# Own loads, own casts, own order: plain fp32 loads on one queue with engine casts, a hand-ordered schedule, and folded weights built in 64x32 PE tiles

## The chip, the cores and the metric

The kernel runs on one core of a Trainium2 chip. The metric is the device time of one execution in microseconds (us), as the median of several executions. A profile covers one execution; its span is about 2 us shorter than the reported time of the same execution (319.5 us of span for 321.31 us before). Engine names: PE is the matrix engine, PEld its weight loads, DVE the vector engine, ACT the scalar engine, POOL the GpSimd engine, SP the engine that only issues DMAs here. A program on one core has no second die to compare with, so a single run is called fast or slow by the other runs of its kernel.

## The reference, cut to what matters

```python
# q, k, v: (8 batches, 8 heads, 576, 64)   p: (8, 8, 32, 64)   all fp32
p_packed = softmax(p k^T / 8) v                  # 32 packed rows per head
x        = softmax(q p_packed^T / 8) p_packed    # (8, 8, 576, 64) -> (4608, 512)
out      = relu(x @ w_in)**2 @ w_out             # w_in 512x2048, w_out 2048x512
```

Both kernels use an identity that makes the rest readable. The second attention has only 32 keys per head, so x @ w_in can be written as a2 @ M. Here a2 holds the 256 softmax columns (8 heads of 32), and M = p_packed @ w_in, folded per head, is 256x2048 for each batch. For each batch the kernels run the attention chain (k transposes, s1, pv, extraction of p_packed, M, s2, norm), then fc1 (a2 @ M, relu, square), then fc2 (the product with w_out). The attention chain of batch b+1 and the fc2 of batch b-1 are merged into the fc1 of batch b.

## The kernel before: the parts that matter

Loads go through the casting DMA queue (issued by POOL, fp32 in memory, bf16 when landed). Only v is loaded as fp32 and cast by POOL.

```python
def load_kqv(b):
    ...
    for qd in range(NQD):
        nc.gpsimd.dma_start(t.k[:, qd, :], quad(k, qd))        # casts on the way
    for jp in range(JP):
        nc.sync.dma_start(t.vf[32 * jp:32 * jp + 32], vv[jp])  # fp32, 32 partitions each
    for qd in range(NQD):
        nc.gpsimd.dma_start(t.q[:, qd, :], quad(q, qd))
...
setup()                               # p, memsets
loads = {0: load_kqv(0)}
for c in range(NWC): load_w_in(c)
loads[1] = load_kqv(1)
for c in range(NWC): load_w_out(c)
```

M is built in pairs of matmuls on two 128x64 halves of the PE array. Each contracts 128 rows with weights that are half zeros.

```python
def m(self, qd, c):
    ps = ps_att.tile([P, 512], F32, name="ps_a", tag="a")
    for pr in range(2):
        nc.tensor.matmul(ps[64 * pr:64 * pr + 64, :], lhsT=self.ppT[:, qd, pr, :],
                         rhs=w_in_b[:, qd * 2 + pr, c * WCH:(c + 1) * WCH], start=True, stop=True)
    # evacuated by ACT (qd 0) or DVE (qd 1), scaled by 1/denominator
```

fc1 is four matmuls, a relu on ACT and a square on DVE.

```python
nc.scalar.activation(r[:].rearrange("p (c n) -> p c n", c=2), ps[:, :, :HALF], ACT.Relu)
nc.vector.tensor_tensor(out=g[:, fb, o:o + S], in0=r, in1=r, op=ALU.mult)
```

The order of instructions on each engine is left to the tool's scheduler. The `merge` function only gives it the program order.

The softmax here doesn't subtract the row's maximum and nothing guards it: scores larger than these inputs give would overflow.

Of the kernel before, what the change touches and what calls it, by code (L numbers as in the profile page):

```python
# [9 lines left out]
F32 = mybir.dt.float32  # L10
# [17 lines left out]
def kernel_impl(tc, q, k, v, p, w_in, w_out, out):  # L28
# [14 lines left out]
    with ExitStack() as ctx:  # L43
        consts = ctx.enter_context(tc.tile_pool(name="consts", bufs=1))
        qkv = ctx.enter_context(tc.tile_pool(name="qkv", bufs=2))
        att = ctx.enter_context(tc.tile_pool(name="att", bufs=2))
        small = ctx.enter_context(tc.tile_pool(name="small", bufs=4))
        mpool = ctx.enter_context(tc.tile_pool(name="mpool", bufs=2))
        rpool = ctx.enter_context(tc.tile_pool(name="rpool", bufs=4))
        opool = ctx.enter_context(tc.tile_pool(name="opool", bufs=4))  # L50
# [6 lines left out]
        w_in_b = consts.tile([P, NCB, DFF], BF16, name="w_in_b")  # L57
# [3 lines left out]
        p_b = consts.tile([P, B * NQD, D], BF16, name="p_b")  # L61
        pT_bd = consts.tile([P, B * NQD, 2, P], BF16, name="pT_bd")
        ppT_bd = [consts.tile([P, NQD, 2, 64], BF16, name=f"ppT_bd{i}") for i in range(2)]
        pq_bd = [consts.tile([P, NQD, 2, P], BF16, name=f"pq_bd{i}") for i in range(2)]

        def load_kqv(b):
            t = Ctx()
            t.k = qkv.tile([P, NQD, JT * D], BF16, name="k_b")
            t.v = qkv.tile([JP * 32, G, H * D], BF16, name="v_b")
            t.vf = qkv.tile([JP * 32, H, G * D], F32, name="v_f")  # L70
            t.q = qkv.tile([P, NQD, JT * D], BF16, name="q_b")

            def quad(src, qd):
                return src[b, qd * QH:(qd + 1) * QH].rearrange("h (a j) d -> (h a) (j d)", j=JT)

            for qd in range(NQD):
                nc.gpsimd.dma_start(t.k[:, qd, :], quad(k, qd))  # L77
            vv = v[b].rearrange("h (a jp g) d -> jp a h (g d)", jp=JP, g=G)
            for jp in range(JP):
                nc.sync.dma_start(t.vf[32 * jp:32 * jp + 32], vv[jp])  # L80
            for qd in range(NQD):
                nc.gpsimd.dma_start(t.q[:, qd, :], quad(q, qd))  # L82
            return t

        def load_w_in(c):
            nc.gpsimd.dma_start(
                w_in_b[:, :, c * WCH:(c + 1) * WCH],
                w_in[:, c * WCH:(c + 1) * WCH].rearrange("(cb p) f -> p cb f", p=P))

        def load_w_out(c):  # L90
            nc.gpsimd.dma_start(
                w_out_b[:, c * 4:(c + 1) * 4, :],
                w_out[c * WCH:(c + 1) * WCH, :].rearrange("(fb p) e -> p fb e", p=P))

        def setup():
            nc.gpsimd.dma_start(p_b, p.rearrange("b (qd h) i d -> (h i) (b qd) d", h=QH))
            nc.vector.memset(pT_bd, 0.0)
            nc.vector.memset(ones_bd, 0.0)
            nc.vector.memset(ones_c, 1.0)
            for h in range(QH):  # L100
                nc.vector.memset(ones_bd[32 * h:32 * h + 32, 32 * h:32 * h + 32], 1.0)
            for i in range(2):
                nc.vector.memset(ppT_bd[i], 0.0)
                nc.vector.memset(pq_bd[i], 0.0)

        def setup_p(b):
            for h in range(QH):
                r = slice(32 * h, 32 * h + 32)
                for qg in range(b * NQD, (b + 1) * NQD):
                    nc.vector.transpose(  # L110
                        pT_bd[r, qg, :, r],
                        p_b[r, qg, :].rearrange("p (dh dl) -> p dh dl", dh=2))

        class Att:
            def __init__(self, b, t):
                self.b, self.t = b, t
                self.kT = att.tile([P, NQD, 2, S], BF16, name="kT")
                self.qT = att.tile([P, NQD, 2, S], BF16, name="qT")
# [4 lines left out]
                self.ppT = ppT_bd[b % 2]  # L123
                self.pq = pq_bd[b % 2]

            def tr_q(self, qd):
                nc.vector.transpose(  # L127
                    self.qT[:, qd].rearrange("p dh (j a) -> p j dh a", a=32),
                    self.t.q[:, qd, :].rearrange("p (j dh dl) -> p j dh dl", dh=2, dl=32))

            def tr_k(self, qd):
                nc.vector.transpose(  # L132
                    self.kT[:, qd].rearrange("p dh (g jp a) -> p jp g dh a", jp=JP, a=32),
                    self.t.k[:, qd, :].rearrange("p (jp g dh dl) -> p jp g dh dl", jp=JP, dh=2, dl=32))

            def cast_v(self, qd):
                nc.gpsimd.tensor_copy(  # L137
                    self.t.v[:, :, qd * QH * D:(qd + 1) * QH * D].rearrange("p g (h d) -> p h g d", d=D),
                    self.t.vf[:, qd * QH:(qd + 1) * QH, :].rearrange("p h (g d) -> p h g d", d=D))

            def s1(self, qd, hf):
                ps = ps_att.tile([P, 512], F32, name="ps_a", tag="a")
                for gi in range(3):
                    g = hf * 3 + gi
                    for dh in range(2):
                        lhsT = self.kT[:, qd, dh, g * 96:(g + 1) * 96]
                        nc.tensor.matmul(ps[:JP * 32, gi * P:(gi + 1) * P], lhsT=lhsT,  # L147
                                         rhs=pT_bd[:, self.b * NQD + qd, dh, :],
# [4 lines left out]
            def pv(self, qd):  # L153
# [3 lines left out]
                c0 = qd * 256  # L157
                for pr in range(2):
                    h0 = qd * QH + 2 * pr
                    for g in range(G):  # L160
# [60 lines left out]
            def steps(self):  # L221
# [3 lines left out]
                for qd in range(NQD):  # L225
                    for hf in range(2):
                        st.append(lambda qd=qd, hf=hf: self.s1(qd, hf))
# [133 lines left out]
```

## Time and profile before

| before | value |
|---|---|
| reported time, median of 4 | 321.25 us (321.07 to 321.68) |
| span of the profile, PE busy | 319.5 us, 80% |
| first M matmul | 56.88 us |
| first relu of fc1, batches 0, 1, 2 | 66.7, 90.5, 116.1 us |
| first relu of fc1, batch 7, and end | 277.0, 319.5 us |

The page of the profile cuts the span into 40 slices of 8.0 us. A digit is a busy share in tenths. The PEclk row is the clock granted to PE in tenths of full speed (it shows 9 also where the trace holds no clock record, here before 63.5 us), and GB/s is what the DMA engines moved.

```profile
PE   0030200889999999999979998999999999999994
...
POOL 7032715141041311130030012000000000000000
PEclk9999999979999999999999999999999999999999
DMA  9999999994097364555442321121111111112232
GB/s 160 198 212 209 213 256 210 240 192 74 3 194 157 61 148 102 135 100 124 112 101 43 96 64 33 34 54 49 34 33 35 33 36 50 48 35 66 52 81 67
```

PE is nearly empty for seven slices while the DMA row is full, then nearly full to the end. The chain of waits (start, length, what) says which loads the first stage waited for:

```profile
4.62 19.37 DMA w_in_b<-in_moe_w_in_dram
24.28 15.86 DMA w_out_b<-in_moe_w_out_dram
40.66 16.19 DMA k_b<-in_k_dram
```

The timeline of DVE shows the second reason for the late start. The transposes of p for later batches stand ahead of batch 0's extraction (the reciprocal):

```profile
38.67 8.52 DVE L110 STREAM_TRANSPOSE pT_bd<-p_b 32x64 bf16<-32x64 bf16 x45
47.22 0.17 DVE L171 RECIPROCAL rD<-ps_pp 128x2 f32<-128x2 f32 x1
```

From the starts of successive matmuls in the trace, the nominal step is 216 ns for a 512-column matmul, 122 for 288, 56 for 128, and 29 for 64. A pair of M matmuls starts 3 ns apart, but the step before it grows from 216 to 309 ns and the step after it is 336 ns. A pair thus costs 309 - 216 + 3 + 336 = 432 ns, about half of which is not streaming. This is as the Trainium skill (TensorEngine Tiling (Array Packing), Key Properties) has it: a change of tiling mode drains the engine.

### The profile page before, as it was taken

How to read it: one execution, taken by the hardware profiler on the slowest of the kernel's cores; microseconds unless marked ns; L12 is line 12 of the kernel's file. 1: busy time of each engine (PE TensorE's matmuls, PEld its weight loads, DVE VectorE, ACT ScalarE, POOL GpSimd, SP SyncE). 2: the span in 40 equal slices, each digit the busy share in tenths (PEclk: the TensorE clock that was granted, in tenths of full speed). 3: DMA queues.
4: the chain of work that ended last, by engine and by line, in shares of the span. 5: the costliest groups of instructions: out<-in, count | busy, mean ns of one | idle time of the engine just before them, and what ended most of it. 6: DMA issues, size and time to landing. Idle time of an engine off the chain costs nothing.

```text
span 319.5 us, 4844 instructions
## 1 busy us (share of the span) xinstructions
PE 256.6 (80%) x1792; PEld 140.4 (44%) x1792; DVE 164.9 (52%) x355; ACT 178.9 (56%) x357; POOL 48.2 (15%) x61
## 2 busy tenths in 40 slices
PE   0030200889999999999979998999999999999994
PEld 0030200256464456445634564546445644455441
DVE  3073894569685966484648464842454245433100
ACT  1020001768887855785579556856785578565211
POOL 7032715141041311130030012000000000000000
PEclk9999999979999999999999999999999999999999
DMA  9999999994097364555442321121111111112232
GB/s 160 198 212 209 213 256 210 240 192 74 3 194 157 61 148 102 135 100 124 112 101 43 96 64 33 34 54 49 34 33 35 33 36 50 48 35 66 52 81 67
DMA packets 24360, 33.09 MB, mean 104 GB/s; under 512 B 5392, under 2 KB 15632, under 8 KB 24336
## 3 DMA queue, kind: packets, MB, share of 16 engines
q0 software_dynamic: 10896, 13.90, 26.3%
q1 hardware_dynamic: 13440, 18.89, 23.9%
q8 instruction: 14, 0.23, 0.3%
q14 instruction: 10, 0.08, 0.1%
HBM read 37.22 MB, written 9.44 MB: 146 GB/s over the span
## 4 chain that ended last, share of the span: by engine, by line
PE 66%; DMA 16%; DVE 8%; ACT 6%; issue 1%; POOL 1%; ACTq 0%; POOLq 0%
PE ps_o L263 34%; PE ps_h L247 17%; PE ps_a L190 7%; DMA w_in_b<-in_moe_w_in_dram 6%; DMA k_b<-in_k_dram 5%; DMA w_out_b<-in_moe_w_out_dram 5%; PE ps_a L147 3%; ACT r L251 3%; DVE gT L253 3%; PE ps_a L203 3%; DVE a_641 L219 1%; PE ps_a L214 1%; PE ps_pp L161 1%; DVE kT L132 1%; DVE qT L127 1%
## 5 line engine op out<-in xcount | busy, mean ns | idle before, releaser
L263 PE MATMUL ps_o<-w_out_b,gT 128*128 128x512 bf16 x576 | 156.3, 380 | 0.0
L251 ACT ACTIVATE r<-ps_h 128x576 bf16<-128x576 f32 x128 | 82.4, 648 | 37.2 <-PE ps_h L247 35.8
L253 DVE TENSOR_TENSOR gT<-r 128x576 bf16<-128x576 bf16 x128 | 59.7, 472 | 67.7 <-ACT r L251 66.9
L263 PEld LDWEIGHTS <-gT 128*128 128x128 bf16 x576 | 52.4, 98 | 44.6 <-issue 8.9
L247 PEld LDWEIGHTS <-M 128*128 128x128 bf16 x512 | 48.4, 98 | 30.5 <-issue 5.5
L197 DVE TENSOR_SCALAR M<-ps_a,rD 128x512 bf16<-128x512 f32 x32 | 24.0, 750 | 22.8 <-PE ps_a L190 22.5
L132 DVE STREAM_TRANSPOSE kT<-k_b 128x1152 bf16<-128x1152 bf16 x16 | 22.0, 1376 | 26.5 <-DMA k_b<-in_k_dram 23.6
L147 PE MATMUL ps_a<-pT_bd,kT 128*96 128x128 bf16 x192 | 17.5, 238 | 20.5 <-DVE pT_bd L110 20.4
L267 ACT COPY o_sb<-ps_o 128x512 f32<-128x512 f32 x36 | 21.0, 584 | 20.4 <-PE ps_o L263 20.1
L137 POOL CAST v_b<-v_f 96x1536 bf16<-96x1536 f32 x16 | 23.8, 1522 | 53.7 <-DMA v_f<-in_v_dram 28.1
L147 PEld LDWEIGHTS <-kT 128*96 128x96 bf16 x192 | 16.2, 138 | 25.0 <-DVE kT L132 19.5
L203 PE MATMUL ps_a<-qT,pq_bd_94 128*128 128x288 bf16 x32 | 7.6, 323 | 22.5 <-ACT pq_bd_94 L183 19.5
L195 ACT ACTIVATE M<-ps_a,rD 128x512 bf16<-128x512 f32 x32 | 22.0, 688 | 5.8 <-PE ps_a L190 5.0
L183 ACT ACTIVATE pq_bd_94<-ps_pp 32x64 bf16<-32x64 f32 x16 | 3.4, 213 | 33.9 <-DVE ppT_bd_92 L174 26.3
L127 DVE STREAM_TRANSPOSE qT<-q_b 128x1152 bf16<-128x1152 bf16 x16 | 21.6, 1362 | 0.6 <-PE ps_a L203 0.6
L190 PE MATMUL ps_a<-w_in_b,ppT_bd_92 128*64 128x512 bf16 x64 | 14.1, 434 | 2.0 <-ACT M L195 1.2
L216 ACT ACTIVATE ls<-ps_a 128x288 f32<-128x288 f32 x32 | 13.4, 418 | 4.0 <-PE ps_a L214 3.5
L218 ACT ACTIVATE rs<-ls 128x288 f32<-128x288 f32 x32 | 14.2, 445 | 0.8
L82 POOL DMA_DIRECT2D q_b<-in_q_dram x16 | 8.5, 536 | 40.8 <-DVE qT L127 33.7
L203 PEld LDWEIGHTS <-pq_bd_94 128*128 128x128 bf16 x32 | 3.0, 101 | 26.2 <-ACT pq_bd_94 L183 21.0
L161 PEld LDWEIGHTS <-v_b 96*128 96x128 bf16 x192 | 8.2, 101 | 13.1 <-POOL v_b L137 11.4
L77 POOL DMA_DIRECT2D k_b<-in_k_dram x16 | 8.5, 536 | 32.9 <-DVE kT L132 23.8
(165 smaller groups left out, 236.3 us busy)
## 6 DMA issues: line engine op xcount, KB each, us to landing
v_f<-in_v_dram SPq DMA_DIRECT2D x24, 384.0 KB, 7.0
out_dram<-o_sb SPq DMA_DIRECT2D x144, 64.0 KB, 1.7
k_b<-in_k_dram POOLq DMA_DIRECT2D x16, 288.0 KB, 13.2
q_b<-in_q_dram POOLq DMA_DIRECT2D x16, 288.0 KB, 9.7
w_in_b<-in_moe_w_in_dram POOLq DMA_DIRECT2D x4, 512.0 KB, 20.3
w_out_b<-in_moe_w_out_dram POOLq DMA_DIRECT2D x4, 512.0 KB, 18.7
p_b<-in_p_dram POOLq DMA_DIRECT2D x1, 256.0 KB, 15.2
```

Of the source, the lines that this page charges most:

```text
L127: nc.vector.transpose(self.qT[:, qd].rearrange("p dh (j a) -> p j dh a", a=32), self.t.q[:, qd, :].rearrange("p (j dh dl) -> p j dh dl", d ...
L132: nc.vector.transpose(self.kT[:, qd].rearrange("p dh (g jp a) -> p jp g dh a", jp=JP, a=32), self.t.k[:, qd, :].rearrange("p (jp g dh dl) ...
L137: nc.gpsimd.tensor_copy(self.t.v[:, :, qd * QH * D:(qd + 1) * QH * D].rearrange("p g (h d) -> p h g d", d=D), self.t.vf[:, qd * QH:(qd + 1 ...
L147: nc.tensor.matmul(ps[:JP * 32, gi * P:(gi + 1) * P], lhsT=lhsT, rhs=pT_bd[:, self.b * NQD + qd, dh, :], start=(dh == 0), stop=(dh == 1))
L190: nc.tensor.matmul(ps[64 * pr:64 * pr + 64, :], lhsT=self.ppT[:, qd, pr, :], rhs=w_in_b[:, qd * 2 + pr, c * WCH:(c + 1) * WCH], start=True ...
L195: nc.scalar.activation(dst, ps, ACT.Copy, scale=self.rD[:, qd:qd + 1])
L197: nc.vector.tensor_scalar_mul(dst, ps, self.rD[:, qd:qd + 1])
L247: nc.tensor.matmul(ps[:, c, :HALF], lhsT=a.M[:, qd, fb * FB:(fb + 1) * FB], rhs=a.a2[:, qd, c * HALF:(c + 1) * HALF], start=(qd == 0), sto ...
L251: nc.scalar.activation(r[:].rearrange("p (c n) -> p c n", c=2), ps[:, :, :HALF], ACT.Relu)
L253: nc.vector.tensor_tensor(out=g[:, fb, o:o + S], in0=r, in1=r, op=ALU.mult)
L263: nc.tensor.matmul(st.ps, lhsT=g[:, fb, n0:n0 + P], rhs=w_out_b[:, fb, :], start=(fb == 0), stop=(fb == NFB - 1))
L267: nc.scalar.copy(o_sb, st.ps)
```

## The change

The intent has four parts. First, start earlier: load only what batch 0 needs first, on one plain queue, in the order of need. Second, since plain loads don't cast, let POOL, ACT and DVE cast. Third, take the order of every engine into one's own hands (`manual_schedule`, with weights for where each list is merged). Fourth, build M in groups of eight matmuls on eight 64x32 tiles (64 rows of contraction, without the zeros), so 32 groups in place of 64 pairs. The q-side scale moves, and the layouts of k and v change so that v can be loaded in two pieces of 96 partitions; for this the k transposes write with a stride of 3 elements.

The core of the diff, cuts marked with `...`:

```diff
+        ctx.enter_context(tc.manual_schedule())
         ...
+            def dma_kq(self, name, qd):
+                src = {"k": k, "q": q}[name]
+                f = stg.tile([P, JT * D], F32, name="kq_f", tag="kq")      # 4 staging buffers
+                nc.sync.dma_start(f, src[self.b, qd * QH:(qd + 1) * QH].rearrange(
+                    "h (a j) d -> (h a) (j d)", j=JT))
         ...
+            def cast_kq(self, name, qd, engs):
+                ...
+                t = qkv.tile([P, JT * D], BF16, name=name + "_b", tag="kqb")
+                for i, e in enumerate(engs):
+                    cast(e, t[:, i * n:(i + 1) * n], f[:, i * n:(i + 1) * n])
         ...
+        def dma_w_out(c):
+            f = stg.tile([P, 2, NE], F32, name="w_f", tag="w", bufs=4)
+            nc.sync.dma_start(f, w_out[c * 2 * P:(c + 1) * 2 * P, :].rearrange("(fb p) e -> p fb e", p=P))
+            w_f[c] = f
+        def cast_w_out(c, eng):
+            cast(eng, w_out_b[:, 2 * c:2 * c + 2, :], w_f[c])
         ...
-                    self.kT[:, qd].rearrange("p dh (g jp a) -> p jp g dh a", jp=JP, a=32),
+                    self.kT[:, qd].rearrange("p dh (g a jp) -> p jp g dh a", jp=JP, a=32),
         ...
-            def m(self, qd, c):
-                ps = ps_att.tile([P, 512], F32, name="ps_a", tag="a")
-                for pr in range(2):
-                    nc.tensor.matmul(ps[64 * pr:64 * pr + 64, :], lhsT=self.ppT[:, qd, pr, :],
-                                     rhs=w_in_b[:, qd * 2 + pr, c * WCH:(c + 1) * WCH],
+            def m(self, c):
+                pss = [ps_att.tile([P, 512], F32, name="ps_a", tag="a") for _ in range(NQD)]
+                for h in range(QH):
+                    for qd in range(NQD):
+                        pr, e = divmod(h, 2)
+                        o = 32 * (h ^ qd)
+                        nc.tensor.matmul(pss[qd][o:o + 32, :], lhsT=self.ppT[64 * e:64 * e + 64, qd, pr, :],
+                                         rhs=w_in_b[64 * e:64 * e + 64, qd * 2 + pr, c * WCH:(c + 1) * WCH],
         ...
+        merge([([lambda fb=fb: fc1_unit(a0, fb) for fb in range(8)], 0, 1), (c1, 0, 1)])
+        cast_w_in(1, 3, V)
+        a0.m(2)
+        a0.m(3)
         ...
+        merge([(pc[4:], 0.0, 0.02), ([s1[4], s1[7]] + s1[8:], 0.0, 0.25), (fst, 0.06, 0.55),
+               ([lambda fb=fb: fc1_unit(a1, fb) for fb in range(NFB)], 0.25, 0.75), (rest, 0.55, 1),
+               (pool_casts(L[2])[:2] + [lambda: prep_p(2, B)] + pool_casts(L[2])[2:], 0.55, 0.7),
+               (a2.steps(), 0.6, 1.0), (L[3].dma_steps(), 0.6, 0.9)])
```

In the last call each list has the stretch (0 to 1) of the merged program in which its steps are spread.

## The prediction

> **What bounds the kernel now.** Two stages. (1) Start-up: in the 40 slices PE is nearly empty until slice 8; the chain of waits is DMA from 4.6 to 56.9 us (w_in 19.4, w_out 15.9, k 16.2 us), and the timeline has the first M matmul at 56.9 us. It is order rather than bandwidth: v of two batches and all of w_out are among the first loads, k lands only at 17.8 us, and the scheduler put 45 transposes of p (8.5 us) and those of batch 1 ahead of batch 0's extraction, which waits until 47.2 us. (2) From 57 us PE: 39 to 40 of 40 us busy per window. Start-to-start times from the trace: fc2 216 ns, fc1 122, s1 56, pv 29. An M pair (128x64 tiles) runs together, but stretches the matmul before it from 216 to 309 ns and needs 336 itself: 432 ns per pair, 27.6 us for 64 pairs, half of it switching. That agrees with the Trainium skill (TensorEngine Tiling (Array Packing), Key Properties): changing the tiling mode drains the engine. PE work is about 30.7 us per batch, 245 in all; ACT and DVE are at 70% and 50%.
>
> **Loads.** The casting queue writes 2304-byte packets in 192 ns, 205 to 210 GB/s written, so some 420 GB/s read. Perfetto Trace Analysis, Roofline, in the skill, gives about 435 for 16 engines: plain fp32 loads read the same bytes and win almost no bandwidth. They win order: p of two batches, k0, v0, q0 and half of w_in are 5.8 MB, an estimated 15 to 17 us. With casts (POOL about 1 ns per element per partition, from the v cast's 1.5 us), transposes (1.4 us) and the extraction, the first M matmul comes at about 21 us (18 to 27). The other weights and batch 1 (about 10 MB, 25 us) land by about 45 us, so up to 50 us PE runs with holes: I allow 8 us. Casts add about 8 us per batch to POOL, which has room.
>
> **M.** 64 pairs become 32 groups of eight 64x32 matmuls on eight different tiles. If all stream together, a group costs 216 + 213 + some loads, about 480 ns: 15 us instead of 27.6. If the two row halves take turns, about 21.
>
> **Sum.** PE work 29.2 us per batch, 233 us, 4 of it before the first M. 21 + 229 + 8 (holes while loading) + 5 (steady holes; before has about 10 there) = 263; + 4.6 from last matmul to the end of the span (as before) - about 2 if hand order is tight; + 1.7 between span and reported time. About **266 us**, range 252 to 281. Faster by over 2%: 0.97; within 2%: 0.02; slower: 0.01. Of the 55 us, 28 are start-up (36 less 8), 12 M, the rest scheduling.
>
> **What would show it.** Timeline: first M at 18 to 27 us; extraction before 18. DMA row: full to about 45 us, 350 to 420 GB/s instead of 200. M: from a group's first matmul to the next instruction near 340 ns rather than 550. PE nearly full from 50 us. ACT busiest after PE, about 80% of steady time.
>
> **What would make it wrong.** Row halves not overlapping (+6 us); the SP queue shared by loads that wait for staging buffers and stores behind them, so an output buffer could hold ACT and then PE; POOL casts slowed by DVE so that k/q come late; both attention PSUM buffers taken by one M group, so each next step waits for the slower of ACT and DVE; w_out later than 45 us.

## More of the kernel before

From the groups of instructions, three lines are needed later. Columns: line, engine, operation, output<-input, shapes, count; then busy us and mean ns; then idle time before them and what ended it.

```profile
L253 DVE TENSOR_TENSOR gT<-r 128x576 bf16<-128x576 bf16 x128 | 59.7, 472 | 67.7 <-ACT r L251 66.9
L132 DVE STREAM_TRANSPOSE kT<-k_b 128x1152 bf16<-128x1152 bf16 x16 | 22.0, 1376 | 26.5 <-DMA k_b<-in_k_dram 23.6
L137 POOL CAST v_b<-v_f 96x1536 bf16<-96x1536 f32 x16 | 23.8, 1522 | 53.7 <-DMA v_f<-in_v_dram 28.1
```

The windows view gives the busy time of each engine in a stretch. The two rows are fc1 of batch 0 to 1 and of batch 1 to 2:

```profile
66.00:90.00 24.00, 23.20 (x180) 13.75 (x179) 17.40 (x36) 19.83 (x42) 5.15 (x7) 0.93 0.42 76
90.00:116.00 26.00, 24.80 (x195) 13.99 (x194) 21.17 (x37) 20.78 (x44) 7.08 (x8) 1.00 0.74 150
```

The columns are window, its length, busy us (and count) of PE, PEld, DVE, ACT and POOL, clock, DMA share, GB/s. PE is busy 23.2 of 24 us and 24.8 of 26 us: once it started, this kernel hardly had holes, even while the second half of the loads was landing.

## The result, and the profile after

| | before | after |
|---|---|---|
| reported time, median (lowest to highest), 4 runs each | 321.25 (321.07 to 321.68) | 309.74 (308.44 to 310.8) |
| ratio of fast runs, 95% interval | 1 | 0.9638 (0.9599 to 0.9677) |
| first M matmul | 56.88 us | 23.75 us |
| first relu of fc1, batches 0, 1, 2 | 66.7, 90.5, 116.1 | 28.7, 69.9, 104.5 |
| first relu of fc1, batch 7, and end of span | 277.0, 319.5 | 263.6, 306.3 |

Ratios here and below are the mean time of one kernel's fast runs over the mean of the other's in the same rounds, so they are not quite the ratio of the medians that I quote.

The direction was right, but the size was not. The change gained 11.5 us where 55 had been predicted, and 309.74 lies above the predicted range of 252 to 281. The same rows of the page after (slices of 7.7 us):

```profile
PE   0647466689687989989999999999999999999993
...
POOL 4443885410369404910492039202940200000000
PEclk9999969579999999999999999999999999999998
DMA  7979998950378259974188216751111121121232
GB/s 251 344 264 342 311 320 298 252 176 0 79 228 245 60 146 277 334 194 144 46 248 264 64 39 189 197 198 35 37 34 36 45 60 35 34 61 44 61 78 69
```

PE works from the second slice on, but up to about the fourteenth slice mostly at four to eight tenths, in three of them at a reduced clock, where before it was full as soon as it started. POOL is busy in bursts.

The start went as predicted. The timeline has the extraction at 15.98 us (before 47.22) and the first M group at 23.75 us. The first of its eight matmuls ran 0.75 us ahead of the other seven, so that this group took 1.37 us:

```profile
15.98 0.17 DVE L227 RECIPROCAL rD<-ps_pp 128x2 f32<-128x2 f32 x1
23.75 1.37 PE L246 MATMUL ps_a<-w_in_b,ppT 64*32 64x512 bf16 x8
```

An undisturbed M group behaves as predicted too. In 12 of the 20 groups after batch 2's fc1 has begun the eight matmuls start 3 ns apart, the step before the group is 309 ns, and the step after it is 319 ns. Such a group of eight costs 309 - 216 + 7 x 3 + 319 = 433 ns, as much as a pair before. In the other 8 the first matmul again runs 22 to 368 ns ahead of the seven: the second needs the group's other PSUM buffer, which is not free yet. Of the ten groups between fc1 of batch 0 and that of batch 2, nine were split like this, by 98 to 2656 ns, 5.7 us in all.

What is new is in the windows, the groups and the waits. First the windows: 28 to 70 us is fc1 of batch 0 to 1, and 70 to 104 us is that of batch 1 to 2. They answer to the two rows above.

```profile
28.00:70.00 42.00, 27.65 (x202) 14.18 (x201) 27.32 (x46) 21.47 (x40) 22.56 (x26) 0.80 0.88 273
70.00:104.00 34.00, 27.54 (x221) 15.32 (x220) 21.28 (x35) 21.68 (x40) 18.17 (x34) 1.00 0.46 129
```

PE was busy 27.65 of 42 us and 27.54 of 34 us. The groups, against those of before:

```profile
L308 DVE TENSOR_TENSOR gT<-r 128x576 bf16<-128x576 bf16 x128 | 74.5, 586 | 65.9 <-ACT r L306 64.8
L188 DVE STREAM_TRANSPOSE kT<-k_b 128x1152 bf16<-128x1152 bf16 x16 | 32.9, 2077 | 0.0
L78 POOL CAST v_b<-v_f 96x1536 bf16<-96x1536 f32 (+1 forms) x16 | 23.4, 1478 | 5.0 <-DMA v_f<-in_v_dram 4.9
```

The squares on DVE grew from 472 to 586 ns on average although their shape is unchanged. The k transposes grew from 1376 to 2077 ns with the strided output. PE's waits (who waited for whom, us in total, times, longest):

```profile
PE ps_a L198 <- DVE kT L188: 18.4, 10, 9.3
PE ps_a L260 <- ACT M L252: 4.3, 9, 0.8
...
PE ps_a L246 <- DVE w_in_b L78: 3.5, 1, 3.5
```

Of the 18.4 us, 9.3 are the wait for PE's very first matmul. The same view for 28.7 to 104.5 us alone, the stretch between fc1 of batch 0 and that of batch 2, begins:

```profile
PE ps_a L198 <- DVE kT L188: 5.1, 3, 2.8
PE ps_a L246 <- DVE ppT L224: 3.7, 2, 2.5
PE ps_a L246 <- DVE w_in_b L78: 3.5, 1, 3.5
PE ps_a L246 <- DVE pq_bd_102 L237: 2.3, 1, 2.3
PE ps_a L260 <- ACT M L252: 1.5, 3, 0.8
```

The view lists 20.6 us of waits in this stretch, and a product of DVE ends 15.6 us of them.

### A ledger of the span

I split each span at the starts of fc1 of batches 0, 2 and 7 (here and below, fc1 of a batch starts with its first relu), and I call a hole what the step from one matmul's start to the next exceeds the nominal step of its shape (216, 122, 56, 29 ns; the members of an M group share one 216, and one-column matmuls count next to nothing). Mode switching and a half clock therefore count as holes. The sum of nominal steps is 228.8 us before and 221.9 us after. I give this only for traces that have all their matmuls; in some of the traces below 26 to 33 fc2 records are missing. The three last columns are experiments that come further down.

| us | before | after | casting DMA, hand order (e18) | casting DMA, scheduler (e20) | the same, M in groups of four (e23) |
|---|---|---|---|---|---|
| start of fc1, batch 0 | 66.7 | 28.7 | 28.4 | 38.7 | 39.2 |
| batch 0 to 2 | 49.4 | 75.8 | 71.4 | 62.1 | 59.3 |
| of which holes | 9.0 | 36.4 | 32.1 | 19.4 | 15.5 |
| batch 2 to 7 | 160.9 | 159.1 | 157.3 | 147.6 | 152.6 |
| of which holes | 16.1 | 18.9 | 17.1 | 11.0 | 10.6 |
| batch 7 to end | 42.5 | 42.7 | 42.9 | 42.9 | 42.9 |
| span | 319.5 | 306.3 | 300.0 | 291.3 | 294.0 |

Read the columns before and after. Up to fc1 of batch 0 the holes fell from 60.9 to 24.2 us, a gain of 36.7, which was the plan. From batch 0 to batch 2 they rose by 27.4 us, and from batch 2 to 7 by 2.8 us. With 6.9 us less nominal work this gives 36.7 - 27.4 - 2.8 + 6.9 = 13.4 us, against 13.2 measured. So the lead of 38.0 us at batch 0 has shrunk to 11.6 us by batch 2. The question for the experiments is what makes the 27 us, and why the steady part, with 20 M groups for 40 pairs, has no fewer holes.

### The profile page after: what moved, and what is told of

Same layout as the page of the kernel before. It is cut to its first block, busy times and chain, and to the rows that moved or that the text cites. A ratio compares the mean times of both kernels' runs of the same rounds, so it can differ in the third digit from the quotient of the medians.

```text
span 306.3 us, 5208 instructions
## 1 busy us (share of the span) xinstructions
PE 255.9 (84%) x1920; PEld 141.5 (46%) x1920; DVE 184.0 (60%) x306; ACT 179.7 (59%) x329; POOL 104.0 (34%) x178
## 4 chain that ended last, share of the span: by engine, by line
PE 49%; DVE 18%; ACT 13%; DMA 8%; issue 4%; SPq 3%; POOL 3%; ACTq 0%; POOLq 0%; DVEq 0%
PE ps_o L319 24%; PE ps_h L302 14%; DVE kT L188 6%; DVE gT L308 5%; ACT r L306 4%; DMA kq_f<-in_q_dram 3%; PE ps_a L246 3%; PE ps_a L198 3%; ACT M L252 3%; SPq L328 3%; PE ps_a L260 2%; ACT o_sb L323 2%; DMA out_dram<-o_sb 2%; DVE qT L183 2%; DMA kq_f<-in_k_dram 2%
## 5 line engine op out<-in xcount | busy, mean ns | idle before, releaser
L319 PE MATMUL ps_o<-w_out_b,gT 128*128 128x512 bf16 x576 | 159.2, 382 | 0.0
L308 DVE TENSOR_TENSOR gT<-r 128x576 bf16<-128x576 bf16 x128 | 74.5, 586 | 65.9 <-ACT r L306 64.8
L319 PEld LDWEIGHTS <-gT 128*128 128x128 bf16 x576 | 54.3, 98 | 46.0 <-issue 11.5
L188 DVE STREAM_TRANSPOSE kT<-k_b 128x1152 bf16<-128x1152 bf16 x16 | 32.9, 2077 | 0.0
L323 ACT COPY o_sb<-ps_o 128x512 f32<-128x512 f32 x36 | 20.8, 581 | 18.4 <-PE ps_o L319 9.7
L246 PE MATMUL ps_a<-w_in_b,ppT 64*32 64x512 bf16 x256 | 20.9, 428 | 12.5 <-DVE ppT L224 3.7
L254 DVE TENSOR_SCALAR M<-ps_a,rD 128x512 bf16<-128x512 f32 x32 | 23.8, 744 | 9.1 <-PE ps_a L246 9.1
L78 POOL CAST v_b<-v_f 96x1536 bf16<-96x1536 f32 (+1 forms) x16 | 23.4, 1478 | 5.0 <-DMA v_f<-in_v_dram 4.9
L235 POOL COPY pq_bd_102<-ppT 32x64 bf16<-32x64 bf16 x24 | 6.0, 250 | 51.8 <-DVE ppT L224 50.8
L78 POOL CAST k_b<-kq_f 128x1152 bf16<-128x1152 f32 (+1 forms) x16 | 18.3, 1162 | 6.7 <-DMA kq_f<-in_k_dram 6.4
L198 PE MATMUL ps_a<-pT_bd_99,kT 128*96 128x128 bf16 x96 | 9.1, 244 | 13.6 <-DVE kT L188 13.6
L235 POOL COPY pq_bd_101<-ppT 32x64 bf16<-32x64 bf16 x24 | 5.9, 245 | 41.4 <-DVE ppT L224 40.4
L78 POOL CAST q_b<-kq_f 128x1152 bf16<-128x1152 f32 (+1 forms) x16 | 19.1, 1210 | 1.2 <-DMA kq_f<-in_q_dram 1.2
L246 PEld LDWEIGHTS <-ppT 64*32 64x32 bf16 x256 | 5.4, 90 | 30.1 <-issue 20.4
```

The source lines that it names most:

```text
L78: eng.tensor_copy(dst, src)
L188: nc.vector.transpose(self.kT[:, qd].rearrange("p dh (g a jp) -> p jp g dh a", jp=JP, a=32), self.t.k[qd][:].rearrange("p (jp g dh dl) -> ...
L198: nc.tensor.matmul(ps[:JP * 32, gi * P:(gi + 1) * P], lhsT=lhsT, rhs=pT_bd[self.b % 2][:, (qd * 2 + dh) * P:(qd * 2 + dh + 1) * P], start= ...
L246: nc.tensor.matmul(pss[qd][o:o + 32, :], lhsT=self.ppT[64 * e:64 * e + 64, qd, pr, :], rhs=w_in_b[64 * e:64 * e + 64, qd * 2 + pr, c * WCH ...
L254: nc.vector.tensor_scalar_mul(dst, pss[e], self.rD[:, e:e + 1])
L319: nc.tensor.matmul(st.ps, lhsT=g[:, fb, n0:n0 + P], rhs=w_out_b[:, fb, :], start=(fb == 0), stop=(fb == NFB - 1))
```

## The experiments

The theories at the start were these:

- Order: the hand-written order on each engine leaves the attention chain of batches 1 and 2 exposed, with PE waiting behind it.
- Bytes: the loads of batches 1 and 2 and of w_out can't keep up with the earlier start.
- Clock: the granted clock is 0.5 at 37 to 44 and at 54 to 65 us, and this itself costs the time.
- M: the grouping is what gained, or is worth nothing.

A fifth theory, that the casts hold up DVE, came only when an experiment went the wrong way (e14). Hand-ordered versions differ by 1 to 2% from run to run, so effects of 1 to 2 us between them are not resolved. Before was run in every job, with medians of 320.8 to 321.5 us.

### e1, before with only the M groups of eight

Edit, on the kernel before:

```diff
-            def m(self, qd, c):
-                ps = ps_att.tile([P, 512], F32, name="ps_a", tag="a")
+            def m(self, c):
+                pss = [ps_att.tile([P, 512], F32, name="ps_a", tag="a") for _ in range(NQD)]
                 ...                                   # as in the change, with its layouts of pT, pq and ppT
-                st += [s2s[0], s2s[1], ms[0], ns[0], s2s[2], ms[1], ns[1], s2s[3], ms[2], ns[2], ms[3], ns[3],
-                       ms[4], ms[5], ms[6], ms[7]]
+                st += [s2s[0], s2s[1], ms[0], ns[0], s2s[2], ns[1], ms[1], s2s[3], ns[2], ms[2], ns[3], ms[3]]
```

> The kernel before, with M alone changed: one group of eight 64x32 matmuls per 512 columns instead of two pairs in 128x64 tiles (and the head order that it needs). Loads, casts and schedule stay. Measured in the changed kernel: one group costs 433 ns of PE (309 + 319 + gaps of 3, less the 216 of the matmul before), where two pairs cost 864, so M alone should save 32 x 0.43 = 13.8 us where PE is full. Theory A (the whole measured gain of 11.5 us is M's, and loads, casts and hand order net nothing, their early start being given back between 24 and 100 us): 307 to 311 us, near the changed kernel's 309.7. Theory B (M's gain is lost in new waits for the two attention PSUM buffers, and the gain comes from the start): 316 us or more.

Measured: 320.76 us (319.23 to 321.32), ratio 0.9991 (0.9933 to 1.005): no gain. In its trace the steady batches are shorter (batch 3 to 7 took 30.75 us each against 31.95), but fc1 of batch 0 starts 1.4 us later, and batch 0 to 1 takes 28.5 instead of 23.8 us. In that stretch DVE stood still on two squares while POOL cast v:

```profile
77.59 3.84 DVE L262 TENSOR_TENSOR gT<-r 128x576 bf16<-128x576 bf16 x2
...
77.86 2.89 POOL L142 CAST v_b<-v_f 96x1536 bf16<-96x1536 f32 x2
```

Two squares in 3.84 us, against 0.47 us each in the kernel before. So in the steady stage the grouping gains 1.2 us per batch (the step times say 8 x 0.432 - 4 x 0.433 = 1.7), and the start loses it again. I did not yet see why those squares were slow.

### e3, the changed kernel with the scheduler free

```diff
-        ctx.enter_context(tc.manual_schedule())
```

> The changed kernel with the scheduler given back its freedom (the line that fixes the hand order is taken out), all else equal. If the hand order of the in-order queues is what loses time between 24 and 100 us (a DVE cast behind eight squares, transposes before the extraction), the scheduler should shorten that stretch: 300 us or less. If the loss is set by when bytes land or by engine speed, the time stays within 3 us of 309.7, and if the hand order is worth what it was written for, it gets slower, 315 or more.

Measured: 298.12 us (294.46 to 300.99), ratio 0.9255 (0.9172 to 0.9337). One line less, and 11.6 us faster than the change. Batch 2 to 7 took 150.8 us against 159.1, batch 0 to 2 74.4 against 75.8. That looks like a gain in the steady stage, but by batch 2 e3 had done six output tiles of fc2 where the change had done four (91 recorded matmuls against 68), so at least 23 x 0.216 = 5.0 us of work had moved forward. Of the 8.3 us some 3 at most belong to the steady stage; most of the gain is fewer holes before batch 2. PE's wait for the k transposes (18.4 us in the change) is 3.4 us here, but this compares unlike things: e3's own first wait, 8.9 us, is put down to the transposed p. Hand order costs time; it doesn't gain any.

### e4, contiguous k transposes again

```diff
-                    self.kT[:, qd].rearrange("p dh (g a jp) -> p jp g dh a", jp=JP, a=32),
+                    self.kT[:, qd].rearrange("p dh (g jp a) -> p jp g dh a", jp=JP, a=32),
```

and v loaded by three DMAs of 32 partitions, as before, which this layout needs.

> The changed kernel with k transposed into the layout of before (contiguous runs of 32 instead of steps of 3 elements), v loaded by three DMAs of 32 partitions for it. Transposes of k should go back from 2.08 to 1.38 us each. PE waits 18.4 us in all for kT, 9.3 of it at the very start. Theory DVE layout: each of the nine later waits loses about 0.7 us, time falls by 4 to 8 us. Rival (the waits are set by the order of the queues, not by the transposes' length): less than 2 us. If v in 32-partition pieces lands later, pv moves and some is given back.

Measured: 308.92 us (305.49 to 312.38), ratio 0.9546 (0.9465 to 0.9628), its profile from a slow run. The fast runs lie some 3 us below the change, and the intervals overlap: not to be told from it. The 701 ns per transpose (2077 - 1376) is real, but the time does not hang on much of it.

### e5, w_out loaded once (wrong on purpose)

```diff
         def dma_w_out(c):
+            if c:
+                w_f[c] = w_f[0]
+                return
```

> The changed kernel with w_out's first 512 KB loaded and cast eight times in place of eight loads: a wrong result on purpose, 3.7 MB less to load before 54 us. Theory DMA (plain loads on one queue deliver w_out and batch 2 too late): time falls by 5 us or more, and the first fc2 matmul comes well before 50 us. Theory queue order (PE reaches the first fc2 at 50.7 us because of the cast of w_in and the transposes on DVE, and by then five of eight chunks are ready): first fc2 stays at 49 to 51 us, time falls by less than 3 us, and that through batch 2's k, v, q landing earlier.

Measured: 314.15 us (309.42 to 315.99), ratio 0.9714 (0.9602 to 0.9825), with two fast runs of four and the profile from a slow one. With seven eighths of w_out (3.7 MB) not loaded, fc1 of batch 1 starts at 71.3 us, no earlier than 69.9. The bytes of w_out are not what holds batch 1 up.

### e6a, e8 and e9: single places in the hand order

e6a gives the last cast of w_in to ACT, ahead of need; e8 loads and casts the rest of p earlier; e9 does both and puts batch 1's pv and extraction before its q transposes.

```diff
-        cast_w_in(1, 3, V)                                             # e6a, e9
+               ([lambda: cast_w_in(1, 3, A)], 0.4, 0.45)])
+        load_p(2, B)                                                   # e8, e9: before the w_out loads
-                    load_p(2, B)
-        merge([(pc[4:], 0.0, 0.02), ([s1[4], s1[7]] + s1[8:], 0.0, 0.25), ...
+        merge([(pc[4:] + [lambda: prep_p(2, B)], 0.0, 0.02), (s1[8:10] + [s1[4], s1[7]] + s1[10:], 0.0, 0.25), ...   # order: e9
```

> The changed kernel with one cast moved: the last piece of w_in goes from DVE, where it stands behind eight squares (landed at 28.7 us, cast from 35.8 to 37.8), to ACT in the middle of those units. Theory queue order: the 3.9 us hole before the third M group goes, fc1 of batch 1 starts at 66 to 67 us instead of 69.9, and the end comes 2 to 4 us earlier. Rival (the stretch is paced by something later, so an earlier third group only waits longer at kT): start of fc1 of batch 1 moves by less than 1 us and the time by less than 1.

> The changed kernel with the rest of p loaded before w_out instead of after batch 2, and cast before the w_out casts. In the changed kernel POOL stands idle from 58.7 to 66.5 us behind this load, and then again behind its transposition, which DVE reaches at 80.4; the casts of batch 2's v and q run at 83 to 89 us though they landed at 60 to 65. Theory queue order on POOL: fc1 of batch 2 starts 4 to 8 us before 104.5, time 302 to 306. Rival (batch 2 is paced by DVE and by the chain of attention steps): fc1 of batch 2 moves by less than 2 us, time within 2 of 309.7.

> Three edits of order in the changed kernel at once: the w_in cast on ACT, batch 1's extraction before its q transposes on DVE (2.6 us), and the rest of p early. Theory queue order: their gains stand one after another in the same chain and add: fc1 of batch 1 at 63 to 65 us, of batch 2 at 90 to 96 us, time 296 to 301 us. Rival: each gain is eaten by the next wait, time 305 or more.

Measured: e6a 310.62 us (306.52 to 329.19), ratio 0.9597 (0.9541 to 0.9652); e8 308.19 (306.05 to 313.01), 0.9578 (0.9531 to 0.9626); e9 308.19 (306.19 to 642.63), 0.9584 (0.9542 to 0.9627). None stands out from 309.74. In e8, whose profile is from a slow run, POOL no longer waits for p, and batch 1 to 2 still takes 34.5 us (34.6 in the change). Each of these waits ended last in the profile, but when it is gone another one ends nearly as late. The run of e9 that was profiled took 642.63 us and is left out of everything: its fc2 matmuls took 825 ns on average, against 382 in the change, and its page has no PEclk row. Why is not known.

### e7, idle matmuls to hold the clock

```diff
+        def warm(ps, n):
+            for _ in range(n):
+                nc.tensor.matmul(ps, lhsT=ones_bd, rhs=warm_b, start=True, stop=True)
                 ps = ps_att.tile([P, 512], F32, name="ps_a", tag="a")
+                warm(ps, {(1, 0, 0): 8, (1, 1, 0): 4}.get((self.b, qd, hf), 0))     # before s1
                 pss = [ps_att.tile([P, 512], F32, name="ps_a", tag="a") for _ in range(NQD)]
+                warm(pss[0], {(0, 2): 16, (1, 0): 24}.get((self.b, c), 0))          # before M
```

> The changed kernel with 52 matmuls added that compute nothing (52 x 216 ns = 11 us warm) at the places where PE waits between 33 and 57 us, so that the granted clock should not fall to half there (it is 0.5 from 37.4 to 44.2 and from 54.4 to 64.7 us). If the half clock is a cause of the slow stretch, 5.1 us of matmul work at half speed, the time falls by 3 to 5 us and the runs scatter less. If it only follows from the waits, less than 1.5 us; if the added matmuls delay the chain, it rises by 1 to 3 us.

Measured: 308.4 us (306.66 to 312.26), ratio 0.959 (0.9544 to 0.9637); the mean granted clock rose from 0.968 to 0.987. The Trainium skill (TensorE: Matmul & The Clock Gate, What's actually happening) says that PE drops to half rate after an idle window of about 3.4 us. The trace of the change agrees in part: the 0.5 stretches begin at 37.4 us, in a wait of 3.5 us, and at 54.4 us, just after a wait of only 2.5 us. With the holes filled by useless matmuls the time stays the same within 2 us. So the half clock follows from the holes and is not what makes them.

### e10, e11, e12: moving the attention of batch 2 forward

e10 takes e9 and spreads fc2 tighter and the chain of batch 2 earlier; e11 is e10 with the scheduler free. e12 is e4 with the scheduler free.

```diff
-               ..., (fst, 0.06, 0.55), ..., (rest, 0.55, 1),
-               (pool_casts(L[2]) ..., 0.55, 0.7), (a2.steps(), 0.6, 1.0), (L[3].dma_steps(), 0.6, 0.9)])
+               ..., (fst, 0.06, 0.40), ..., (rest, 0.45, 1),
+               (pool_casts(L[2]), 0.40, 0.45), (a2.steps(), 0.42, 0.95), (L[3].dma_steps(), 0.6, 0.95)])
```

> The three order edits and one more: batch 2's attention steps begin in the middle of batch 1's fc1 instead of near its end (and their casts before them, and fc2's second pair of tiles a little earlier). In the changed kernel and in the run with p early alike, fc1 of batch 1 to fc1 of batch 2 took 34.5 us, with p there or not: 20 us of fc1 with fc2, then 14 us in which the attention steps run one after another with nearly nothing for PE beside them. Theory overlap (the hand order puts a batch's chain of attention steps after the previous batch's fc1 in the first three batches, so PE has no other work while it waits): fc1 of batch 2 at 94 to 99 us, time 299 to 303. Rival (the chain's own speed, or POOL and DVE, set the pace): fc1 of batch 2 above 102, time above 305.

> The same order given to the scheduler as its priorities, not fixed. The changed kernel with a free scheduler took 298.1 us against 309.7: it did six fc2 tiles by 103 us where the hand order did four, and its later batches took 30.1 us each instead of 31.2. If the start and the later batches add, 290 to 295 us. If the scheduler finds the same overlap whatever the order, 297 to 299.

> The changed kernel with the scheduler free and k's transposes in contiguous runs (1.38 us instead of 2.08). With the hand order that layout was worth about 1 us at most. With the free scheduler, DVE takes 15% of the chain between 24 and 104 us for k's transposes and 14% for squares: if DVE paces that stretch, the time falls by 3 us or more from 298.1; if PE's lack of ready work does, less than 1.5.

Measured: e10 305.53 us (303.14 to 309.63), ratio 0.9513 (0.9475 to 0.955): better than the change by about 4 us. fc1 of batch 2 starts at 97.5 instead of 104.5 us, so the chain of batch 2 had indeed been exposed; half of this goes again at once, because batch 2 to 3 then takes 37.5 instead of 34.3 us. e11: 301.5 (297.24 to 306.47), 0.9365 (0.9315 to 0.9416), no better than e3, so with a free scheduler the written order of this part hardly matters. e12: 326.53 (323.98 to 329.78), 1.0145 (1.0101 to 1.0188), slower by 28 us than e3, from which it differs only in the k and v layout. I have no explanation for it. It shows that the scheduler's result can jump with a small change, so e3 and e20 below are single results and no law about schedulers.

### e14, batch 1 without loads (wrong on purpose)

```diff
+        landed = dict(L[0].k), dict(L[0].vf), dict(L[0].q)
         ...
-        for f in L[1].dma_steps():
-            f()
+        L[1].k, L[1].vf, L[1].q = landed              # and w_out loaded once, as in e5
```

> The changed kernel in which batch 1 casts batch 0's landed k, v and q again and w_out is loaded once: 7.2 MB less to land before 54 us, every cast and every step of compute kept; a wrong result on purpose. In the changed kernel fc1 of batch 0 starts at 28.7 us, of batch 1 at 69.9, of batch 2 at 104.5. Theory DMA (the slow first batches wait for bytes): fc1 of batch 1 at 60 us or earlier. Theory order (they wait for their own chain of steps in in-order queues): fc1 of batch 1 at 67 to 71 us, time within 3 us of 309.

Measured: 317.82 us (316.54 to 319.76), ratio 0.9899 (0.9836 to 0.9961): with 7.2 MB fewer to load it is 8 us slower than the change. The theory of bytes wanted fc1 of batch 1 at 60 us or earlier; it starts at 80.6. Without PE's wait of 13.6 us (below) that would be an estimated 67 us, and the change without its own wait of 3.5 us for the same cast an estimated 66: these bytes give nothing. The trace shows why it is slower. Since all data is there, POOL casts without a pause from 32.4 to 47.3 us. Over the same time this is DVE, then POOL, from the timeline, then PE's wait:

```profile
32.25 0.46 DVE L311 TENSOR_TENSOR gT<-r 128x576 bf16<-128x576 bf16 x1 [0.22 <-ACT r L309]
32.89 14.68 DVE L311 TENSOR_TENSOR gT<-r 128x576 bf16<-128x576 bf16 x4 [0.18 <-ACT r L309]
47.49 0.68 DVE L78 CAST w_in_b<-w_f 128x1024 bf16<-128x1024 f32 x1
```

```profile
33.66 3.10 POOL L78 CAST v_b<-v_f 96x1536 bf16<-96x1536 f32 x2
36.71 2.23 POOL L78 CAST q_b<-kq_f 128x1152 bf16<-128x1152 f32 x2
38.89 8.37 POOL L78 CAST w_out_b<-w_f 128x1024 bf16<-128x1024 f32 x8
...
PE ps_a L249 <- DVE w_in_b L78: 13.6, 1, 13.6
```

A square takes 0.46 us; the next four take 14.68 us, one of them alone 11.21 us (from 33.95 to 45.16), during which ten POOL casts start one after another. Behind them DVE's cast of w_in comes at 47.49, and PE waits 13.6 us for it. The Trainium skill (SBUF — State Buffer, Who interferes with whom) names a mechanism that fits: a DVE instruction with two SBUF inputs contends with a GpSimd instruction that reads SBUF, and whoever holds the shared ports blocks the other for the whole instruction. The square has two SBUF inputs. The trace agrees, and goes further, since the waiting DVE instruction was passed by many POOL instructions and not by one.

The same is then seen in the change. Its timeline at the wait for w_in_b (3.5 us above):

```profile
34.12 1.77 DVE L308 TENSOR_TENSOR gT<-r 128x576 bf16<-128x576 bf16 x2 [0.34 <-ACT r L306]
34.12 1.46 POOL L78 CAST k_b<-kq_f 128x1152 bf16<-128x1152 f32 x1
35.53 1.69 POOL L78 CAST v_b<-v_f 96x1536 bf16<-96x1536 f32 x1
35.81 1.95 DVE L78 CAST w_in_b<-w_f 128x1024 bf16<-128x1024 f32 x1
37.82 0.61 PE L246 MATMUL ps_a<-w_in_b,ppT 64*32 64x512 bf16 x3 [3.55 <-DVE w_in_b L78]
```

The cast of w_in, 0.68 us when POOL was quiet, took 1.95 us beside a POOL cast. Taken over the whole trace: of the 160 two-input DVE operations (128 squares and 32 products of norm) 54 overlap a POOL instruction and take 840 ns on average; the others take 455. The excess over 455 ns adds up to 20.8 us in the change, 5.3 us before, and 32.5 us in e14.

### e15, e3 with M later

```diff
-                       ... ms[0], s2s[0], s2s[1], ms[1], ns[0], s2s[2], ns[1], ms[2], s2s[3], ns[2], ms[3], ns[3], nop]
+                       ... s2s[0], s2s[1], ms[0], ns[0], s2s[2], ns[1], s2s[3], ns[2], ms[1], ns[3], ms[2], ms[3], nop]
```

> The scheduler free and one more edit: three of the four M groups of a batch after its softmax steps, so that the softmax does not wait for the two PSUM buffers that an M group takes. If those buffers cost what the waits of s2 and norm for M show in the changed kernel (7 to 8 us over the run), the time falls by 2 to 5 us from the 298.1 of the free scheduler alone. If not, within 1.5 us of it.

Measured: 306.81 us (301.29 to 309.36), ratio 0.9452 (0.9374 to 0.953). Four of the six runs are slow ones, as is the profile; by the ratios of fast runs it is slower than e3 by about 6 us. The order of M and s2 in the change was thus a good one for the scheduler too. Why the difference is so large stays open.

### e17, batch 1 without attention (wrong on purpose)

```diff
         a1 = Att(1, L[1])
-        s1 = a1.steps()
+        a1.M, a1.a2 = a0.M, a0.a2
+        s1 = [nop] * len(a1.steps())
```

The casts for batch 1 stay.

> The changed kernel with batch 1's attention taken out (its fc1 uses batch 0's M and weights; loads and casts of batch 1 stay): a wrong result on purpose. It takes 5.3 us of matmul work away. Theory exposed chain (from 41 to 70 us PE mostly waits for that chain, with 13 fc2 matmuls beside it): fc1 of batch 1 starts 14 to 20 us earlier, at 50 to 56 us, far more than the work that is taken away, and the end comes 10 us or more earlier. Rival (the time is only moved, as by the edits of order): fc1 of batch 1 earlier, but the end earlier by 7 us or less.

Measured: 296.93 us (295.75 to 299.05), ratio 0.9261 (0.9209 to 0.9313). fc1 of batch 1 starts at 47.8 us, 22.1 us earlier, and the span is 12.3 us shorter (306.3 - 294.0). The work removed is about 5.3 us: 221.9 - 217.5 = 4.4 us of nominal steps, and four M switches of 0.22 us. So some 7 us of the holes belong to the exposed chain of batch 1. The other 10 us of the early arrival are lost to batch 2, which then takes 45.0 instead of 34.6 us to reach its fc1. The waits between 48 and 93 us say what held it:

```profile
PE ps_a L198 <- DVE kT L188: 13.0, 1, 13.0
DVE pT L102 <- POOL p_b L78: 10.1, 1, 10.1
POOL p_b L78 <- DMA p_f<-in_p_dram: 7.6, 1, 7.6
```

PE stands still for 13.0 us until batch 2's k is transposed. On DVE this comes after the transposition of p, which waits for POOL's cast of p, which waits for the load of p, queued behind batch 2's k, v and q. So here the late place of one load ended last. In the change batch 2 arrives later, and there an earlier p alone gave nothing (e8).

### e18 and e20: the engine casts undone

e18 is the change with its order, its M, its hand schedule, but with the casting DMA queue for k, q, w_in and w_out. v and p are still cast by the engines. e20 is e18 with the scheduler free.

```diff
-                f = stg.tile([P, JT * D], F32, name="kq_f", tag="kq")
-                nc.sync.dma_start(f, src[self.b, qd * QH:(qd + 1) * QH].rearrange(
+                f = qkv.tile([P, JT * D], BF16, name=name + "_b", tag="kqb")       # 12 buffers
+                nc.gpsimd.dma_start(f, src[self.b, qd * QH:(qd + 1) * QH].rearrange(
         ...
         def cast_w_out(c, eng):
-            cast(eng, w_out_b[:, 2 * c:2 * c + 2, :], w_f[c])
+            pass                                      # w_in, k and q likewise
-        ctx.enter_context(tc.manual_schedule())       # e20 only
```

> The changed kernel with the loads part undone: k, q, w_in and w_out are again cast by the DMA on the POOL queue, as before the change; the hand order, the M groups and v's load with its POOL cast stay. Found since: a DVE square (two inputs in SBUF) does not run while POOL casts, and POOL's casts come back to back: squares take 20.8 us more than 455 ns each allows (5.3 in the kernel before), and when the w_out loads and batch 1's loads were taken away, POOL cast for 13.6 us on end and one square took 11.2 us. Theory contention (casts on POOL hold up DVE, and through it PE): squares' excess falls under 10 us, batches 3 to 6 take 30.3 us or less each instead of 31.2, and the end comes 4 to 10 us before 309.7, though the first M comes some us later. Rival (exposed chain and order alone): 308 or more.

> As the run with casting DMAs, with the scheduler free. The free scheduler alone took 298.1. If contention and order are two separate losses, 288 to 295 us, the best of the study. If casting DMAs cost the start what they give later, 296 to 300.

Measured: e18 301.87 us (301.13 to 303.66), ratio 0.9415 (0.9378 to 0.9452); e20 291.31 us (288.97 to 293.12), ratio 0.9058 (0.9016 to 0.9101). e20 beats both kernels. With e3 and the change the four make a table (medians):

| | hand order | scheduler | hand order costs |
|---|---|---|---|
| engine casts | 309.7 (the change) | 298.1 (e3) | 11.6 |
| casting DMA | 301.9 (e18) | 291.3 (e20) | 10.6 |
| engine casts cost | 7.8 | 6.8 | |

The two costs are nearly additive, each known to some 2 us. The squares in e18 and then e20, and POOL's row of e20, to be set against the change:

```profile
L300 DVE TENSOR_TENSOR gT<-r 128x576 bf16<-128x576 bf16 x128 | 65.7, 518 | 70.0 <-ACT r L298 69.2
```

```profile
PE   0154389798979999999999999999999999999993
...
POOL 9343933936253137012700270003000200000000
...
L299 DVE TENSOR_TENSOR gT<-r 128x576 bf16<-128x576 bf16 x128 | 63.0, 502 | 63.3 <-ACT r L297 62.6
```

586 ns per square in the change, 518 in e18, 502 in e20. The excess over 455 ns falls from 20.8 to 9.8 and 8.3 us. In e3 it is 18.4 us and a square takes 580 ns, nearly as in the change, although e3 is 11.6 us faster: the free scheduler gains elsewhere. More differs in e18 than POOL's casts: it has no fp32 staging buffers for these loads, so a load no longer waits for one, the loads leave on another queue, and the casts of k, q and the weights on ACT and DVE are gone too. How much of the 7 to 8 us is DVE's waiting was not separated; no run moved POOL's casts to ACT alone.

The ledger above shows something more. e20 starts fc1 of batch 0 at 38.7 us, 10 us later than e18, and reaches batch 2 at 100.8 us against 99.8, with more fc2 done on the way. For the arrival at batch 2, ten microseconds of an earlier start were worth nothing here, though the order differs as well.

### e22, e18 with the forward move of e10

The edit is that of e10, on e18.

> Casting DMAs with the hand order in which batch 2's attention begins in the middle of batch 1's fc1 (305.5 us with POOL casts). If the two gains add, 296 to 301 us; if not, 303 to 306.

Measured: 301.28 us (298.54 to 303.61), ratio 0.9361 (0.9314 to 0.9409). fc1 of batch 2 starts at 98.9 us (e18 99.8); the steady part stays that of a hand order. The 4 us of e10 are not had a second time, which suggests that they and the casts were partly the same wait.

### e23, e20 with M in groups of four

```diff
-            def m(self, c):
-                pss = [ps_att.tile([P, 512], F32, name="ps_a", tag="a") for _ in range(NQD)]
+            def m(self, qd, c):
+                ps = ps_att.tile([P, 512], F32, name="ps_a", tag="a")
                 for h in range(QH):
-                    for qd in range(NQD):
+                    ...                               # one qd: 64 groups of four, one PSUM buffer each
```

> The best kernel so far (casting DMAs, scheduler free, 291.3 us) with the M group of eight undone into two groups of four 64x32 tiles, each with one PSUM buffer and its own evacuation: 64 groups instead of 32. A group of four should switch and stream like a group of eight, 433 ns less what is shared, so 32 more of them cost 13.8 us of PE, of which 1 to 2 us may be hidden in the start. Theory: the saving of M groups is real where no other wait takes it: 301 to 305 us. Rival (as in the kernel before with M alone changed: the two buffers that a group holds cost what it saves): within 3 us of 291.3.

Measured: 293.64 us (293.27 to 296.24), ratio 0.9155 (0.9114 to 0.9195): 2.3 us slower than e20, in another job, so known to about 2 us. A group of four still costs 309 and 319 ns around it, so 32 more groups are 32 x 0.433 = 13.9 us more of PE's time, of which 6.9 us (228.8 - 221.9) are nominal steps. The ledger shows where they went. The holes are fewer by 4.3 us in e23 (3.9 in batch 0 to 2, 0.4 in batch 2 to 7) although 32 more switches, an estimated 6.9 us (32 x 0.216), are in them. So about 11 us of other waiting in e20 disappear when M is cut finer. In this pair of programs, the grouping of eight turns most of what it saves into waits.

## Why the prediction was right or wrong

**Right: the start.** "the first M matmul comes at about 21 us (18 to 27)": 23.75. "extraction before 18": 15.98. The diagnosis of before, order rather than bandwidth, holds, and the first M matmul came 33.1 us earlier (predicted "36").

**Nearly right: the loads.** "350 to 420 GB/s instead of 200" in the DMA row: 251 to 344 in the first seven slices, below the range. That the plain queue reads hardly faster was right: the Trainium skill's figure of about 435 GB/s for 16 engines (Perfetto Trace Analysis, Roofline) is about what the q pieces reach, 590 KB each, which land 1.2 to 1.5 us after the piece before (some 390 to 490 GB/s), but the 96-partition v pieces of the same size need 2.3 to 3.3 us. "The other weights and batch 1 ... land by about 45 us": the last w_out landed at 53.3 us. The prediction listed this lateness among the dangers, but in e5 and e14 nothing is won when these bytes are not loaded.

**Wrong: "up to 50 us PE runs with holes: I allow 8 us".** This is the step that failed, and with it "PE nearly full from 50 us". From batch 0 to 2 there are 36.4 us of holes, 12.0 of them up to 50 us and 24.4 after it; without an estimated 2 us of M switching, which the prediction counted as work, 34 us for the 8. I had asked only whether data would be there. Most of the data was there in time; what wasn't was the chain from it, and DVE's part of it above all (15.6 of the 20.6 us of listed waits). e17 shows about 7 us for the attention of batch 1 alone, e10 about 4 us for batch 2, and e18 4.4 us for the casts in this stretch (75.8 - 71.4). Not the cause, as far as tested: the bytes of batch 1 and w_out (e5, e14), clock (e7), single places in the order (e6a, e8, e9). These parts do not add up to the whole: even e20, the best, still has 19.4 us of holes there and starts 10 us later. I can say that an early start isn't kept unless the chains of batches 1 and 2 move with it; the last 10 to 15 us of these holes are not assigned.

**Wrong: "Casts add about 8 us per batch to POOL, which has room".** POOL had room: it was busy for 104 of 306 us. The failing thought is that busy time is all that a cast costs. POOL and DVE share ports, and the casts held up the squares, which lie between fc1 and fc2, and DVE's own casts. The engine casts cost 6.8 to 7.8 us in time (e20 against e3, e18 against the change). Among the dangers I had named the opposite direction, "POOL casts slowed by DVE". That DVE is held up is shown by the traces; that this, and not the staging buffers, is what makes those 7 us is argued.

**Wrong in size: "12 M".** The mechanism was right: groups of eight run together at 433 ns (predicted about 480), and PE's step sum fell. But the gain in time was not to be told from zero in before (e1, 320.76 against 321.3 us) and 2.3 us in e20 (against e23). The danger was named, "both attention PSUM buffers taken by one M group, so each next step waits for the slower of ACT and DVE", and it came: in the change PE's waits for evacuations of M add up to 9.5 us (4.3 of them for ACT's in s2), where before they were 2.6 us together.

**Wrong: "5 (steady holes; before has about 10 there)" and "about 2 if hand order is tight".** From batch 2 to 7 the holes are 18.9 us, and without 20 switches of 0.217 us still 14.6; in before 16.1 - 40 x 0.216 = 7.5. The hand order cost 10.6 to 11.6 us against the scheduler on the same program (e3, e20). How much of that is in this steady part is best read from e18 and e20, whose traces are complete: there the steady holes fall from 17.1 to 11.0, so 6.1 us, where the prediction had expected a gain.

Together: about 26 us for the holes up to batch 2, 9.6 for those after it, 2.75 for the first M matmul, and 2 for the bonus of the hand order make some 40 of the 43.7 us between 266 and 309.74.

**Open.** Why e12 and e15 are so much slower than e3; how the 7 us of the engine casts divide between DVE's waiting and the staging buffers; the unassigned holes up to batch 2; why single repairs don't add.

## What to carry to other kernels

Before you count a stage's head start as gained, ask what the next stages wait for: here 38 us of lead at batch 0 were 11.6 us at batch 2, because the chains of batches 1 and 2 stayed where they were. An engine with room is not free if another engine shares its ports: look for an operation whose mean time grows while its shape stays the same (472 to 586 ns here). Such growth shows a wait, and not what the wait costs: e3 kept 580 ns and was 11.6 us faster. A hand order has to be tested against the scheduler on the same program, by deleting one line; and the best version here (291.31 us) keeps the new load order and the new M, leaves casting to the DMA and leaves the order to the scheduler.

## What the Trainium skill lacked or had wrong

- SBUF — State Buffer, Who interferes with whom: the rule speaks of one instruction that blocks the other. It lacks that a queue of GpSimd casts without gaps can keep a DVE instruction waiting over many of them: one square of 0.46 us took 11.21 us while ten casts started (e14). Otherwise the trace agrees.
- TensorEngine Tiling (Array Packing), Key Properties: that switching drains is right, but there is no size. Here the step into a group is 309 ns instead of 216 and the step out 319 to 336, so an undisturbed group of 512 columns costs 432 to 433 ns, whether it has two or eight matmuls.
- VectorE: DVE Perf Modes, The three transpose paths: nothing on the output's stride. The same 128x1152 bf16 transpose took 1376 ns with contiguous and 2077 ns with stride-3 output.
- DMA: Bandwidth & Descriptors: no figure that fits the 96-partition loads with rows of 1536 bytes, 590 KB in 2.3 to 3.3 us, where the q pieces, 128 partitions with rows of 4.6 KB, took 1.2 to 1.5 us.
- TensorE: Matmul & The Clock Gate, Seeing it yourself: it warns that clock records can't always be trusted. Here they can be missing, and the views then show 1.0: the execution of 642.63 us (e9), with fc2 matmuls of 825 ns, has no clock record and a mean clock of 1.000, and in the change, whose first record is at 30.6 us, the M matmuls at 24 us took 602 to 606 ns (387 later) where the views give 1.00. Whether a record can be wrong, no run here shows.
